# A sliding-window attention with a slot mixture of experts, rewritten with long DMA rows, 96-query blocks and experts in column tiles

## The chip, the cores and the metric

One core of one Trainium2 chip runs the whole program. The metric is the device time of one execution in microseconds (us). An execution is called slow when it lies over 1.5% above the fastest one of the same kernel; verdicts of faster and slower use the other, fast ones. Engines are named as the profile does: PE is the matrix engine, PEld its weight loads, ACT the scalar engine, DVE the vector engine, POOL the engine that issues the casting loads here, SP the one that issues the plain ones. In these kernels PE writes its results to a memory called PSUM, and ACT and DVE carry them from there to SBUF, the working memory of 128 partitions.

## The reference

Eight batches of eight heads with 576 tokens of 64 numbers go through causal attention with a window. Heads 0 to 3 (called plain) see the 32 last tokens, heads 4 to 7 (called dilated) see every fourth of the 128 last. The result, 4608 rows of 512, goes through a soft mixture of experts with 32 slots.

```python
scores = scale * np.matmul(q, k.transpose(0, 1, 3, 2))
mask_plain = (rel >= 0) & (rel < 32)
mask_dil   = (rel >= 0) & (rel < 128) & (rel % 4 == 0)
...                                  # softmax over the masked row, then @ v -> x
logits = x @ phi                     # 4608 x 32
slot_input = softmax(logits, axis=0).T @ x
h = relu(slot_input[e] @ w1[e]);  slot_out[e] = h @ w2[e]      # 8 experts of 4 slots
out = softmax(logits, axis=1) @ slot_out
```

## The kernel before

It works on units of two heads. A load puts token `96 c + p` into partition `p`, so each packet is one token of one head: 256 bytes in HBM, 128 as bf16. PE transposes six 96-token pieces of q and of k, ACT copies each result of 576 columns to SBUF.

```python
# st_dmas: k casts to bf16 on the way in, one token per packet
g.dma_start(kbs[:, :, 64*hx:64*hx+64], k[b, h, 0:576, :].rearrange("(c p) d -> p c d", p=96))
...
# st_transposes and st_evacs, once per unit for q and for k
for c in range(NCH):
    last = pe.transpose(psX_bf[:, 96*c:96*c+96], srcb[:, c, :], ident[0:96, 0:96])
...
ac.activation(dst[:, :], psX_bf[:, 0:S], ACTF.Copy)          # 576 columns, dense
```

After all 32 units come a pass over x for the router (transposes, logits, exponentials, slot sums), a step that scales the token weights, the eight experts one after the other, and the output.

The softmax here doesn't subtract the row's maximum and nothing guards it: scores larger than these inputs give would overflow.

Of the kernel before, what the change touches and what calls it, by code (L numbers as in the profile page):

```python
# [11 lines left out]
N_TOK = B * S  # L13
DM = H * D
E_EXP = 8
SLOTS_PER_E = 4
N_SLOTS = E_EXP * SLOTS_PER_E
FF = 1024
SCALE = 1.0 / (D ** 0.5)
N_TT = N_TOK // 128  # L20
N_G = 9
N_KT = 5

_DBG_UNITS = 0
_DBG_STAGE = 0


class SyncEnv:
# [20 lines left out]
    def now(self, eng):  # L49
        et = eng.engine  # L50
        return (self.ctr_sem[et], self.ctr_val[et])

    def waits(self, eng, evs):
        et = eng.engine
        best = {}
        for ev in evs:
            if ev is None:
                continue
            if isinstance(ev, list):
                sub = ev  # L60
            else:
                sub = [ev]
            for sem, val in sub:
                if val <= 0:
                    continue
                key = sem.num
                if key not in best or val > best[key][1]:
                    best[key] = (sem, val)
        for key, (sem, val) in best.items():
            hw = self.hwm.get((et, key), 0)  # L70
            if val <= hw:
                continue
            eng.wait_ge(sem, val)
            self.hwm[(et, key)] = val


class DmaSem:
# [5 lines left out]
    def inc(self, inst, n=16):  # L83
        inst.then_inc(self.sem, n)
        self.val += n
        return (self.sem, self.val)

    def ev(self):
        return (self.sem, self.val)

    def finals(self):
        return [(self.sem, self.val)] if self.val > 0 else []


class Slot:

    __slots__ = ("ready", "reads")

    def __init__(self):
        self.ready = []  # L100
        self.reads = []

    def war(self):
        return list(self.reads) + list(self.ready)

    def written(self, ev):
        self.ready = [ev] if not isinstance(ev, list) else list(ev)
        self.reads = []


def bass_dilated_sliding_attn__then__soft_moe_slots_kernel(
# [8 lines left out]
    dbg_x=None,  # L120
):
    es = ExitStack()
    A = es.enter_context

    env = SyncEnv(nc)
    WT = env.waits
    SIG = env.sig

    x_sb = A(nc.sbuf_tensor("x_sb", [128, N_TT, DM], BF16))
    xT = A(nc.sbuf_tensor("xT", [128, DM // 128, N_TOK], BF16))  # L130
    w1b = A(nc.sbuf_tensor("w1b", [128, E_EXP, DM // 128, FF], BF16))
    phi_st = A(nc.sbuf_tensor("phi_st", [128, DM // 128, N_SLOTS], F32))
    phi_sb = A(nc.sbuf_tensor("phi_sb", [128, DM // 128, N_SLOTS], BF16))
    ident = A(nc.sbuf_tensor("ident", [128, 128], BF16))
    ident_f = A(nc.sbuf_tensor("ident_f", [N_SLOTS, N_SLOTS], F32))
    mask_plA = A(nc.sbuf_tensor("mask_plA", [128, 448], BF16))
    mask_plB = A(nc.sbuf_tensor("mask_plB", [128, 512], BF16))
    mask_dA = A(nc.sbuf_tensor("mask_dA", [128, 512], BF16))
    mask_dB = A(nc.sbuf_tensor("mask_dB", [128, 512], BF16))

    ps_sc = [A(nc.psum_tensor(f"ps_sc{i}", [128, 512], F32)) for i in range(4)]
    ps_pv = [A(nc.psum_tensor(f"ps_pv{i}", [128, 512], F32)) for i in range(2)]
    ps_ta = A(nc.psum_tensor("ps_ta", [128, 512], F32))
    ps_tb = A(nc.psum_tensor("ps_tb", [128, 512], F32))
    ps_ta_bf = ps_ta[:].bitcast(BF16)
    ps_tb_bf = ps_tb[:].bitcast(BF16)

    att_es = ExitStack()
    AA = att_es.enter_context
    mtmp0 = AA(nc.sbuf_tensor("mtmp0", [128, 512], F32))  # L150
    mtmp1 = AA(nc.sbuf_tensor("mtmp1", [128, 512], BF16))
    mtmp2 = AA(nc.sbuf_tensor("mtmp2", [128, 512], BF16))
    NSLOT = 3
    NVS = 6
    NCH = S // 96
    qs = [AA(nc.sbuf_tensor(f"qs{i}", [96, NCH, 128], F32)) for i in range(NSLOT)]
    qb = [AA(nc.sbuf_tensor(f"qb{i}", [96, NCH, 128], BF16)) for i in range(2)]
    kb = [AA(nc.sbuf_tensor(f"kb{i}", [96, NCH, 128], BF16)) for i in range(NSLOT)]
    vb = [AA(nc.sbuf_tensor(f"vb{i}", [128, 2, 5, D + 1], BF16)) for i in range(NVS)]
    QT = [AA(nc.sbuf_tensor(f"QT{i}", [128, S], BF16)) for i in range(2)]  # L160
    KT = [AA(nc.sbuf_tensor(f"KT{i}", [128, S], BF16)) for i in range(2)]
    NPAR = 6
    pte = [AA(nc.sbuf_tensor(f"pte{i}", [128, 512], BF16)) for i in range(2 * NPAR)]
    pt = [AA(nc.sbuf_tensor(f"pt{i}", [128, 512], BF16)) for i in range(2 * NPAR)]
    rinv = [AA(nc.sbuf_tensor(f"rinv{i}", [128, 8], F32)) for i in range(NPAR)]

    s_in = [DmaSem(nc, f"s_in{i}") for i in range(NSLOT)]
    s_vv = [DmaSem(nc, f"s_vv{i}") for i in range(NVS)]
    s_qs = [DmaSem(nc, f"s_qs{i}") for i in range(NSLOT)]
    s_w1 = DmaSem(nc, "s_w1")  # L170
    s_xT = DmaSem(nc, "s_xT")
    s_phi = DmaSem(nc, "s_phi")
    s_w2 = [DmaSem(nc, f"s_w2_{i}") for i in range(3)]
    s_out = [DmaSem(nc, f"s_out{i}") for i in range(6)]

    blk = A(nc.Block())

    sl_qs = [Slot() for _ in range(NSLOT)]
    sl_qb = [Slot() for _ in range(2)]
    sl_kb = [Slot() for _ in range(NSLOT)]  # L180
    sl_vb = [Slot() for _ in range(NVS)]
    sl_QT = [Slot() for _ in range(2)]
    sl_KT = [Slot() for _ in range(2)]
    sl_pta = Slot()
    sl_ptb2 = Slot()
    sl_pte = [Slot() for _ in range(2 * NPAR)]
    sl_pt = [Slot() for _ in range(2 * NPAR)]
    sl_sc = [Slot() for _ in range(4)]
    sl_pv = [Slot() for _ in range(2)]
    sl_rinv = [Slot() for _ in range(NPAR)]  # L190
    sl_w1 = Slot()
    sl_phi = Slot()
    sl_ident = Slot()
    sl_mask_pl = Slot()
    sl_mask_dl = Slot()

    ev_iota = [None]

    @blk.gpsimd
    def _(g):  # L200
        e0 = SIG(g, g.memset(ident[:], 0.0))
        WT(g, [e0])
        ev_id = SIG(g, g.affine_select(out=ident[:], in_=ident[:],
                                      compare_op=AluOp.not_equal, fill=1.0, base=0,
                                      pattern=[[-1, 128]], channel_multiplier=1))
        WT(g, [ev_id])
        ev_id = SIG(g, g.tensor_copy(ident_f[:, :], ident[0:N_SLOTS, 0:N_SLOTS]))
        sl_ident.written(ev_id)
        ev_iota[0] = SIG(g, g.iota(mtmp0[:], [[1, 512]], base=256, channel_multiplier=-1,
                                   allow_small_or_imprecise_dtypes=True))  # L210
        for i in range(NVS):
            ev = SIG(g, g.memset(vb[i][:, :, :, :], 1.0))
            sl_vb[i].written(ev)
        ins = g.dma_start(phi_st[:], moe_phi.rearrange("(c p) s -> p c s", p=128))
        evp = s_phi.inc(ins)
        WT(g, [evp])
        evc = SIG(g, g.tensor_copy(phi_sb[:], phi_st[:]))
        sl_phi.written(evc)

    @blk.vector  # L220
    def _(vv):
        ev = None
        for pb in ps_sc + ps_pv + [ps_ta, ps_tb]:
            ev = SIG(vv, vv.memset(pb[:], 0.0))
        for s_ in sl_sc + sl_pv + [sl_pta, sl_ptb2]:
            s_.written(ev)
        if _DBG_STAGE:
            SIG(vv, vv.memset(x_sb[:], 0.0))
        WT(vv, [ev_iota[0]])
        e2 = SIG(vv, vv.tensor_scalar(mtmp1[:, 0:192], mtmp0[:, 0:192], 287.0, None, op0=AluOp.is_le))  # L230
        e3 = SIG(vv, vv.tensor_scalar(mtmp2[:, 0:192], mtmp0[:, 0:192], 256.0, None, op0=AluOp.is_ge))
        WT(vv, [e2, e3])
        e4 = SIG(vv, vv.tensor_tensor(mtmp1[:, 0:192], mtmp1[:, 0:192], mtmp2[:, 0:192], AluOp.mult))
        e5 = SIG(vv, vv.memset(mask_plA[:], 0.0))
        e6 = SIG(vv, vv.memset(mask_plB[:], 0.0))
        WT(vv, [e4, e5, e6])
        SIG(vv, vv.tensor_copy(mask_plA[:, 0:160], mtmp1[:, 0:160]))
        SIG(vv, vv.tensor_copy(mask_plA[:, 256:416], mtmp1[:, 0:160]))
        SIG(vv, vv.tensor_copy(mask_plB[:, 0:160], mtmp1[:, 0:160]))
        SIG(vv, vv.tensor_copy(mask_plB[:, 256:416], mtmp1[:, 0:160]))  # L240
        evm = SIG(vv, vv.tensor_copy(mask_plB[0:64, 448:512], mtmp1[0:64, 0:64]))
        sl_mask_pl.written(evm)
        WT(vv, [evm] + sl_ident.ready)
        e8 = SIG(vv, vv.memset(mtmp2[:, 0:256], 0.0))
        e9 = SIG(vv, vv.memset(mtmp1[:, 0:256], 0.0))
# [812 lines left out]
```

## Time and profile before

The median of the first runs was 307 us.

| stage of the kernel before | us | bound by |
|---|---|---|
| start and attention, 32 units | 0 to 183 | arrival of k (and v, q) |
| router | 183 to 218 | PE |
| token weights | 218 to 230 | a chain DVE-PE-DVE |
| experts | 230 to 275 | a chain PE-ACT-PE-DVE |
| output | 275 to 307 | eviction and store |

From the page of the kernel before: busy time by engine, then digits of busy time in tenths for 40 equal slices (PEclk is the granted clock of PE in tenths), and the count of DMA packets.

```profile
PE 208.0 (68%) x2188; PEld 125.2 (41%) x2188; DVE 172.1 (56%) x460; ACT 143.0 (47%) x271; POOL 143.3 (47%) x204
...
ACT  1134848747458566484673827453002334322440
...
PEclk9999999999999999999999999999955999995555
DMA  5899999999999999999999005980000499918896
GB/s 124 69 182 154 196 158 164 185 156 179 169 156 193 156 166 184 156 186 162 158 191 143 6 2 75 196 140 2 0 1 2 65 187 202 207 23 308 322 363 239
DMA packets 131197, 45.56 MB, mean 148 GB/s; under 512 B 115024, under 2 KB 123216, under 8 KB 131168
```

DMA is full (9) through slice 22, but moves mostly 150 to 196 GB/s; seven packets in eight are under 512 bytes. The chain that ended last, in shares of the span, by engine and then by line:

```profile
DMA 40%; PE 31%; POOL 11%; DVE 8%; issue 5%; ACT 3%; ACTq 0%; POOLq 0%; DVEq 0%
DMA kb<-in_k_dram 35%; PE ps_pv L904 5%; DMA out_dram<-ostg 5%; PE ps_sc L852 4%; POOL vb L365 4%; PE ps_pv L499 4%; PE ps_pv L739 3%; POOL w1b L374 2%; POOL kb L358 2%; DVE x_sb L528 2%; PE ps_sc L657 2%; PE ps_sc L826 2%; PE ps_tb L401 2%; PE ps_sc L689 2%; PE ps_sc L436 2%
```

Last, busy time by stage (stretch, its length, then busy us and count of PE, PEld, DVE, ACT and POOL, granted clock, DMA share, GB/s):

```profile
23.00:183.00 160.00, 115.83 (x1587) 84.67 (x1587) 124.87 (x338) 98.27 (x185) 109.14 (x149) 1.00 1.52 155
183.00:218.00 35.00, 31.21 (x277) 17.50 (x273) 13.06 (x39) 15.83 (x36) 2.68 (x3) 1.00 0.57 91
218.00:230.00 12.00, 4.71 (x32) 2.61 (x32) 6.45 (x12) 0.00 (x0) 0.00 (x0) 0.65 0.00 1
230.00:275.00 45.00, 37.41 (x232) 14.68 (x232) 2.44 (x11) 14.07 (x24) 4.37 (x5) 0.90 0.73 117
275.00:308.00 33.00, 16.24 (x36) 3.79 (x36) 11.83 (x18) 9.88 (x18) 6.51 (x12) 0.52 0.74 287
```

### The profile page before, as it was taken

The page shows a single profiled execution, that of the slowest core. Times are in us where ns is not written, and L with a number is a line of the kernel's source. Part 1 is how long each engine was busy: PE and PEld are TensorE (multiplying, and loading weights), DVE is VectorE, ACT ScalarE, POOL GpSimd, SP SyncE. Part 2 cuts the span into 40 slices and gives each one's busy share as a digit, 9 for nine tenths or more (in the row PEclk, how much of TensorE's full clock was granted, in tenths as well). Part 3 has the DMA queues.
Part 4 walks back from the last instruction along what each step waited for, and adds up shares of the span by engine and source line. Part 5 has one row for each costly group of instructions (what it writes and reads, how often), then busy time and mean ns, then how long its engine had stood idle before and what let it go on. Part 6 is the DMA issues. An engine that isn't in the chain of part 4 may idle for free.

```text
span 307.3 us, 5998 instructions
## 1 busy us (share of the span) xinstructions
PE 208.0 (68%) x2188; PEld 125.2 (41%) x2188; DVE 172.1 (56%) x460; ACT 143.0 (47%) x271; POOL 143.3 (47%) x204
## 2 busy tenths in 40 slices
PE   0214958669399595794893969988359898856660
PEld 0102736447267364572563757444132333321110
DVE  8622869959679789496894995332530000023441
ACT  1134848747458566484673827453002334322440
POOL 7998959759479696595990003000000212001221
PEclk9999999999999999999999999999955999995555
DMA  5899999999999999999999005980000499918896
GB/s 124 69 182 154 196 158 164 185 156 179 169 156 193 156 166 184 156 186 162 158 191 143 6 2 75 196 140 2 0 1 2 65 187 202 207 23 308 322 363 239
DMA packets 131197, 45.56 MB, mean 148 GB/s; under 512 B 115024, under 2 KB 123216, under 8 KB 131168
## 3 DMA queue, kind: packets, MB, share of 16 engines
q0 software_dynamic: 89824, 29.44, 82.4%
q1 hardware_dynamic: 39616, 12.59, 25.1%
q10 hardware_dynamic: 1728, 3.15, 2.7%
q8 instruction: 18, 0.29, 0.4%
q14 instruction: 11, 0.09, 0.1%
HBM read 61.93 MB, written 9.44 MB: 232 GB/s over the span
## 4 chain that ended last, share of the span: by engine, by line
DMA 40%; PE 31%; POOL 11%; DVE 8%; issue 5%; ACT 3%; ACTq 0%; POOLq 0%; DVEq 0%
DMA kb<-in_k_dram 35%; PE ps_pv L904 5%; DMA out_dram<-ostg 5%; PE ps_sc L852 4%; POOL vb L365 4%; PE ps_pv L499 4%; PE ps_pv L739 3%; POOL w1b L374 2%; POOL kb L358 2%; DVE x_sb L528 2%; PE ps_sc L657 2%; PE ps_sc L826 2%; PE ps_tb L401 2%; PE ps_sc L689 2%; PE ps_sc L436 2%
## 5 line engine op out<-in xcount | busy, mean ns | idle before, releaser
L452 ACT ACTIVATE pte<-ps_sc 128x512 bf16<-128x512 f32 (+1 forms) x128 | 65.9, 584 | 28.7 <-PE ps_sc L436 28.7
L358 POOL DMA_DIRECT2D kb<-in_k_dram x64 | 49.4, 790 | 27.6 <-PE ps_tb L401 27.5
L528 DVE TENSOR_TENSOR x_sb<-ps_pv,rinv 64x320 bf16<-64x320 f32 (+1 forms) x128 | 58.3, 456 | 4.2
L499 PE MATMUL ps_pv<-vb,pt 128*64 128x65 bf16 (+1 forms) x928 | 51.9, 249 | 2.5 <-DVE x_sb L528 2.5
L401 PE MATMUL ps_tb<-ident,kb 96*128 96x96 bf16 x192 | 21.5, 279 | 45.3 <-DMA kb<-in_k_dram 45.0
L365 POOL DMA_DIRECT2D vb<-in_v_dram x64 | 49.1, 783 | 2.1 <-PE ps_sc L436 1.8
L630 POOL DMA_DIRECT2D w2r<-in_moe_w_dram x8 | 7.1, 884 | 90.5 <-PE ps_ta L879 66.1
L499 PEld LDWEIGHTS ps_pv<-vb,pt 128*64 128x64 bf16 (+1 forms) x928 | 40.8, 150 | 13.8 <-DVE x_sb L528 3.2
L415 ACT ACTIVATE KT<-ps_tb 128x576 bf16<-128x576 bf16 x32 | 21.5, 671 | 34.1 <-PE ps_tb L401 34.1
L436 PE MATMUL ps_sc<-QT,KT 64*128 64x160 bf16 (+3 forms) x320 | 33.3, 342 | 4.0 <-ACT KT L415 2.3
L401 PEld LDWEIGHTS ps_tb<-ident,kb 96*128 96x128 bf16 x192 | 15.8, 138 | 48.9 <-DMA kb<-in_k_dram 48.9
L401 PE MATMUL ps_ta<-ident,qb 96*128 96x96 bf16 x192 | 21.1, 277 | 13.0 <-DVE qb L386 13.0
L415 ACT ACTIVATE QT<-ps_ta 128x576 bf16<-128x576 bf16 x32 | 21.5, 671 | 11.6 <-PE ps_ta L401 11.6
L436 PEld LDWEIGHTS ps_sc<-QT,KT 64*128 64x128 bf16 (+1 forms) x320 | 17.3, 126 | 19.2 <-issue 9.7
L519 DVE RECIPROCAL rinv<-ps_pv 128x5 f32<-128x5 f32 x64 | 12.1, 188 | 22.7 <-PE ps_pv L499 21.8
L1010 POOL DMA_DIRECT2D out_dram<-ostg x12 | 6.5, 544 | 38.0 <-ACT ostg L994 33.8
L889 DVE COPY hT<-ps_ta 128x32 bf16<-128x32 bf16 x8 | 1.4, 174 | 35.9 <-PE ps_ta L879 35.9
L863 ACT ACTIVATE h_sb<-ps_sc 4x512 bf16<-4x512 f32 x12 | 7.0, 586 | 30.9 <-PE ps_sc L852 30.9
L368 POOL DMA_DIRECT2D vb<-in_v_dram x32 | 20.5, 641 | 0.0
L401 PEld LDWEIGHTS ps_ta<-ident,qb 96*128 96x128 bf16 x192 | 14.4, 133 | 15.0 <-issue 12.9
L386 DVE CAST qb<-qs 96x768 bf16<-96x768 f32 x32 | 19.2, 602 | 0.8 <-DMA qs<-in_q_dram 0.8
L467 DVE TENSOR_TENSOR pt<-pte,mask_plA 128x448 bf16<-128x448 bf16 x32 | 12.3, 384 | 11.9 <-ACT pte L452 11.6
(103 smaller groups left out, 268.7 us busy)
## 6 DMA issues: line engine op xcount, KB each, us to landing
qs<-in_q_dram SPq DMA_DIRECT2D x64, 144.0 KB, 9.1
w1b<-in_moe_w_dram POOLq DMA_DIRECT2D x8, 1024.0 KB, 11.8
w2r<-in_moe_w_dram POOLq DMA_DIRECT2D x8, 1024.0 KB, 11.4
kb<-in_k_dram POOLq DMA_DIRECT2D x64, 72.0 KB, 11.6
vb<-in_v_dram POOLq DMA_DIRECT2D x64, 64.0 KB, 11.5
out_dram<-ostg SPq DMA_DIRECT2D x12, 256.0 KB, 2.8
out_dram<-ostg ACTq DMA_DIRECT2D x12, 256.0 KB, 3.3
out_dram<-ostg POOLq DMA_DIRECT2D x12, 256.0 KB, 3.1
```

Of the source, the lines that this page charges most:

```text
L358: ins = g.dma_start(kbs[:, :, 64 * hx:64 * hx + 64], k[b, h, 0:576, :].rearrange("(c p) d -> p c d", p=96))
L365: ins = g.dma_start(vbb[:, hx, 0:4, 0:D], v[b, h, 0:512, :].rearrange("(c p) d -> p c d", p=128))
L368: ins = g.dma_start(vbb[0:64, 0:2, 4, 0:D], v[b, h0:h0 + 2, 512:576, :].rearrange("h p d -> p h d"))
L386: ev = SIG(vv, vv.tensor_copy(qb[tpar][:, :, :], qs[slot][:, :, :]))
L401: last = pe.transpose(psX_bf[:, 96 * c:96 * c + 96], srcb[:, c, :], ident[0:96, 0:96])
L415: ev = SIG(ac, ac.activation(dst[:, :], psX_bf[:, 0:S], ACTF.Copy))
L436: inst = pe.matmul(o_ap, lhsT, rhs, start=True, stop=True)
L452: ev = SIG(ac, ac.activation(hc["pteb"][bi][:, 0:wc], hc["scb"][bi][:, 0:wc], ACTF.Exp, scale=SCALE))
L467: ev = SIG(vv, vv.tensor_tensor(hc["ptb"][bi][:, 0:wc], hc["pteb"][bi][:, 0:wc], mk[:, 0:wc], AluOp.mult))
L499: last = pe.matmul(o_ap, lhsT, rhs, start=(ji == 0), stop=(ji == len(js) - 1))
L528: evn = SIG(vv, vv.tensor_tensor(dst, src, rb, AluOp.mult))
L904: last = pe.matmul(psX[0:SLOTS_PER_E, 0:DM], hT[ep][:, cc, :], w2r[ri][:, cc, :], start=(cc == 0), stop=(cc == 7))
```

## The change

The intent: loads in rows of 6 KB instead of packets of 256 bytes, the router inside the attention loop one batch behind, all experts' weights on chip before they are needed, and each expert in a column tile of 32 so that PE can run several at once.

To get 6 KB rows, 24 neighbouring tokens of a head must lie in one partition. Token `24 p + c` sits in partition `p`, column `c`. A transposition of column `c` then yields tokens 24 apart side by side, and the copy from PSUM has to put them back in order.

```diff
-ins = g.dma_start(kbs[:, :, 64 * hx:64 * hx + 64],
-                  k[b, h, 0:576, :].rearrange("(c p) d -> p c d", p=96))
+res.append(g.dma_start(
+    stg[p0:p0 + NPP, s, 0:6144].rearrange("p (g x) -> p g x", g=4),
+    src[b, half::2, :, :].rearrange("h (p c) d -> p h (c d)", c=PCH)))
 ...
-    last = pe.transpose(psX_bf[:, 96 * c:96 * c + 96], srcb[:, c, :], ident[0:96, 0:96])
-ev = SIG(ac, ac.activation(dst[:, :], psX_bf[:, 0:S], ACTF.Copy))
+def st_A(g, r):                       # four times per half batch, r = 0..3
+    for c1 in range(6):
+        for hx in range(2):
+            i_ = t.transpose(pbf[64 * hx:64 * hx + 64, 128 * c1:128 * c1 + NR],
+                             src[0:NR, 2 * typ + hx, 4 * c1 + r, :], ident[0:NR, 0:NR])
+    pv = pbf[:, 0:768].rearrange("x (c h u) -> x c h u", c=6, h=2)
+    if typ == 0:                      # plain heads: token order
+        d = d.rearrange("x h (p c r) -> x r c h p", c=6, r=4)[:, r]
+    else:                             # dilated heads: the four residues one after the other
+        d = d.rearrange("x h (r p c) -> x r c h p", r=4, c=6)[:, r]
+    ac.activation(d, pv[:, :, :, PCH * t:PCH * t + NPP], ACTF.Copy)
 ... (v the same in st_V; scores, masks, PV in blocks of 96 queries and 128 keys)
+ac.activation(expP[:].rearrange("p (r h s) -> p h s r", r=4, h=2),      # router, per batch
+    lg[:, :, 0:288].rearrange("p h (s r) -> p h s r", r=4), ACTF.Exp)
 ... (first layer: four experts in four column tiles; outputs as rows of 4 KB)
```

## The prediction

> **What bounds it now.** The page gives 307 us. Until 183 us the bound is arrival of q/k/v: the chain of waits is 35% "DMA kb<-in_k_dram", and one k load takes 11.6 us from issue to landing. Of 131,197 DMA packets 115,024 are under 512 B; the 40 slices show DMA at 9 but only 150-195 GB/s. A batch (four units of 5 us) takes 20 us. The Trainium skill, "DMA: Bandwidth & Descriptors", Specifications, asks for 512 B or more; the trace agrees so far as the later weight loads, in large rows, reach 196 GB/s of bf16. By windows: 183-218 us is the router pass (35 us, DMA nearly idle, PE 31 us busy), 218-230 token weights (12), 230-275 the experts one after the other (45), 275-307 output (32).
>
> **Removed.** Small packets; the separate router pass (now inside the attention loop, one batch behind); the token-weight stage (now in the output eviction); the expert-by-expert ping-pong.
>
> **Added per batch, from durations in the trace.**
> - ACT: 34 copies or exponentials, costed from 448 columns = 541 ns and 512 = 599 ns: 288 columns 0.40 us, 576 0.66. 24x0.40 + 10x0.66 = 16.4 us, some 18 with gaps.
> - DVE: four evictions of 768 (0.56), eight mask products (0.45), four reciprocals and normalisations (0.23 + 0.95), four XT copies, one ET copy: 13.5 us, 15 with gaps.
> - PE: about 35 groups of small matmuls. Two 64-column tiles run together (L499: two per 54 ns), a 96-wide transposition costs 80 ns, two 64-row tiles 133 ns, and a change of tile shape costs about 190 ns once (seen between L499, L436 and L401). The skill, "TensorEngine Tiling (Array Packing)", Key Properties, says that changing tiling mode drains the engine; the trace agrees. Sum about 21 us, a third of it group starts and drains.
> - DMA: 2.8 MB as bf16 per batch with one expert of w1; at the 150-200 GB/s seen, 14-19 us.
>
> So the loop turns from DMA-bound to bound by PE with ACT close behind; with two or three PSUM buffers I expect 22-24 us per batch, router included (before 20 + 4.4).
>
> **Sum.** First q/k behind w1's first megabyte and a first transposing step: loop starts at 22 us. 16 steps of 11.3 us: 202. Last batch's router: 212. Tail: first layer 4-5 us if four column tiles overlap (14 if not), ReLU, transposes and row sums 5, second layer 64 matmuls at 216 ns = 14 us (each expert's eight share one column tile, so no overlap), output 9.4 MB at the 320-360 GB/s seen = 28 us. Tail 52 against 89 now. The sum is 264; some waits will overlap: predicted **260 us**, 8 in 10 between 228 and 290. Faster by over 2%: 0.90; within 2%: 0.06; slower: 0.04.
>
> Most of the gain is the tail (37 us).
>
> **What would show it.** Right: packets under 512 B near none; DMA digits of 5-8 in the loop; PE over 85% busy there, its waits short and on ACT or DVE; a batch of 22-24 us; the second layer 14 us; output at DMA 8-9.
>
> **Wrong if:** loads onto only 24 partitions run well under 150 GB/s, so that the loop still waits on DMA (then PE waits on stg, 25 us or more a batch); strided ACT or DVE copies cost more than contiguous ones; PSUM ring waits chain PE-ACT-PE (loop over 26 us a batch); or, the other way, PE overlaps better and ACT sets 18 us a batch (about 225 us).

## More of the kernel before

The two groups of ACT that bring q and k to SBUF, with `xcount | busy us, mean ns of one | idle before`:

```profile
L415 ACT ACTIVATE QT<-ps_ta 128x576 bf16<-128x576 bf16 x32 | 21.5, 671 | 11.6 <-PE ps_ta L401 11.6
L415 ACT ACTIVATE KT<-ps_tb 128x576 bf16<-128x576 bf16 x32 | 21.5, 671 | 34.1 <-PE ps_tb L401 34.1
```

## The result and the profile after

| | median us | runs | ratio to the kernel before, 95% interval |
|---|---|---|---|
| before | 307.35 | 306.93 to 309.76 | |
| changed | 387.78 | 387.31 to 388.03 | 1.2593 (1.2528 to 1.2658) |

A ratio here is the mean time of one kernel's fast runs over that of the other's of the same rounds, so it isn't quite the ratio of the medians. The changed kernel is slower by 26%; the prediction was 260 us, and its range ended at 290. The page of the changed kernel, the same lines as before:

```profile
PE 230.0 (60%) x3056; PEld 170.5 (44%) x3056; DVE 140.6 (36%) x242; ACT 297.6 (77%) x302; POOL 54.5 (14%) x108
...
ACT  1398999799979997999799978997899764120660
...
PEclk9999999999999999999999999999999999999995
DMA  7999994059005900599055005600660066000599
GB/s 138 217 205 213 218 208 90 3 90 205 2 2 83 205 8 2 85 218 205 8 91 95 2 2 108 111 2 0 110 113 2 0 110 111 0 2 2 210 405 364
DMA packets 12623, 40.89 MB, mean 106 GB/s; under 512 B 3633, under 2 KB 3633, under 8 KB 10545
```

The loads did what was wanted. There are 12,623 packets instead of 131,197, they run at 205 to 218 GB/s, where the attention part of the kernel before had 155 in the mean (one slice of it reached 196, so the prediction's 196 alone says little), and DMA then stands idle for one or two slices at a time. ACT took its place: 7 to 9 in every slice of the loop, 298 us busy instead of 143. The chain says the same, 52% ACT and 2% waiting for k:

```profile
ACT 52%; PE 20%; issue 15%; DVE 7%; DMA 2%; POOL 0%; ACTq 0%
ACT VT L378 17%; ACT KT L352 13%; ACT QT L352 12%; ACT PT L419 8%; PE ps_2 L339 2%; DMA stg<-in_k_dram 2%; PE ps_0 L651 2%; DVE XB L447 2%; DVE w1r L676 2%; PE ps_0 L339 2%; PE ps_2 L394 2%; ACT expP L486 1%; PE ps_0 L459 1%; PE ps_0 L599 1%; PE ps_1 L670 1%
```

The ACT groups behind it:

```profile
L378 ACT ACTIVATE VT<-ps_2 128x288 bf16<-128x288 bf16 x30 | 40.9, 1634 | 0.0
L352 ACT ACTIVATE KT<-ps_0 128x288 bf16<-128x288 bf16 x26 | 40.0, 1539 | 0.0
...
L352 ACT ACTIVATE QT<-ps_0 128x288 bf16<-128x288 bf16 x26 | 33.3, 1281 | 14.3 <-PE ps_0 L339 13.8
...
L486 ACT ACTIVATE expP<-ps_0 128x576 bf16<-128x576 f32 x4 | 10.3, 2575 | 0.0
```

The groups are split by PSUM buffer, so the K copies stand there three times in full. A copy has 288 columns now, half of the 576 that took 671 ns, and yet it is listed with 1.3 to 1.7 us. These durations include waiting behind the instruction in front, so starts are the better measure. A stretch of ACT's timeline in the loop (start us, us, what):

```profile
132.69 1.86 ACT L352 ACTIVATE KT<-ps_2 128x288 bf16<-128x288 bf16 x1
134.00 1.02 ACT L419 ACTIVATE PT<-ps_1 128x576 bf16<-128x576 f32 x1
134.89 1.51 ACT L352 ACTIVATE QT<-ps_1 128x288 bf16<-128x288 bf16 x1
135.84 1.87 ACT L352 ACTIVATE KT<-ps_1 128x288 bf16<-128x288 bf16 x1
```

From start to start, a plain Q copy takes 0.95 us (134.89 to 135.84), a K copy 1.3 (132.69 to 134.00); in the trace's dilated copies the medians are 0.73 and 0.97. The prediction had 0.40 for each. By stage (columns as before; the first line is three batches of the loop, then the first layer with its transposes and row sums, the second layer, the output):

```profile
102.00:218.00 116.00, 76.77 (x1080) 60.49 (x1078) 42.10 (x75) 106.40 (x107) 15.98 (x28) 1.00 0.44 83
343.00:350.00 7.00, 6.15 (x107) 3.19 (x100) 1.07 (x3) 1.04 (x3) 0.00 (x0) 1.00 0.00 0
350.00:358.50 8.50, 8.16 (x71) 3.84 (x68) 0.69 (x2) 0.00 (x0) 0.00 (x0) 1.00 0.01 2
358.50:386.00 27.50, 10.75 (x36) 2.15 (x36) 13.14 (x19) 12.03 (x18) 0.00 (x0) 0.82 0.86 343
```

Three batches take 116 us, 38.6 each, and ACT is busy for 106 of them. The prediction had 22 to 24 us per batch. The tail is 43 us (343 to 386), where the prediction had 52 and the kernel before takes 89.

One more reading needs no experiment. The four runs of the changed kernel were granted 0.99, 0.71, 0.72 and 0.60 of PE's clock, and took 387.3, 387.8, 388.0 and 387.7 us. PE at 60% of its clock changes nothing, so PE does not bound the loop of this kernel.

### The profile page after: what moved, and what is told of

Same layout as the page of the kernel before. It is cut to its first block, busy times and chain, and to the rows that moved or that the text cites. A ratio compares the mean times of both kernels' runs of the same rounds, so it can differ in the third digit from the quotient of the medians.

```text
span 385.6 us, 7144 instructions
## 1 busy us (share of the span) xinstructions
PE 230.0 (60%) x3056; PEld 170.5 (44%) x3056; DVE 140.6 (36%) x242; ACT 297.6 (77%) x302; POOL 54.5 (14%) x108
## 2 busy tenths in 40 slices
DMA packets 12623, 40.89 MB, mean 106 GB/s; under 512 B 3633, under 2 KB 3633, under 8 KB 10545
## 4 chain that ended last, share of the span: by engine, by line
ACT 52%; PE 20%; issue 15%; DVE 7%; DMA 2%; POOL 0%; ACTq 0%
ACT VT L378 17%; ACT KT L352 13%; ACT QT L352 12%; ACT PT L419 8%; PE ps_2 L339 2%; DMA stg<-in_k_dram 2%; PE ps_0 L651 2%; DVE XB L447 2%; DVE w1r L676 2%; PE ps_0 L339 2%; PE ps_2 L394 2%; ACT expP L486 1%; PE ps_0 L459 1%; PE ps_0 L599 1%; PE ps_1 L670 1%
## 5 line engine op out<-in xcount | busy, mean ns | idle before, releaser
L352 ACT ACTIVATE QT<-ps_0 128x288 bf16<-128x288 bf16 x26 | 33.3, 1281 | 14.3 <-PE ps_0 L339 13.8
L422 DVE TENSOR_TENSOR PT<-PT,mask_d 128x576 bf16<-128x576 bf16 x32 | 14.7, 459 | 73.9 <-ACT PT L419 73.8
L378 ACT ACTIVATE VT<-ps_2 128x288 bf16<-128x288 bf16 x30 | 40.9, 1634 | 0.0
L352 ACT ACTIVATE KT<-ps_0 128x288 bf16<-128x288 bf16 x26 | 40.0, 1539 | 0.0
L419 ACT ACTIVATE PT<-ps_0 128x576 bf16<-128x576 f32 x32 | 26.2, 820 | 12.8 <-PE ps_0 L413 12.8
L419 ACT ACTIVATE PT<-ps_1 128x576 bf16<-128x576 f32 x32 | 26.4, 826 | 11.4 <-PE ps_1 L413 11.4
L352 ACT ACTIVATE KT<-ps_2 128x288 bf16<-128x288 bf16 x20 | 33.3, 1667 | 0.0
L469 DVE COPY XT<-ps_0 128x576 bf16<-128x576 bf16 x15 | 14.8, 983 | 47.8 <-PE ps_0 L459 47.8
L339 PE MATMUL ps_0<-ident,stg 112*64 112x112 bf16 x312 | 20.1, 300 | 17.1 <-DMA stg<-in_k_dram 15.1
L352 ACT ACTIVATE KT<-ps_1 128x288 bf16<-128x288 bf16 x18 | 28.8, 1602 | 0.0
L352 ACT ACTIVATE QT<-ps_2 128x288 bf16<-128x288 bf16 x20 | 27.8, 1388 | 0.7
L422 DVE TENSOR_TENSOR PT<-PT,mask_p 128x576 bf16<-128x576 bf16 x32 | 14.9, 467 | 32.6 <-ACT PT L419 32.6
L394 PE MATMUL ps_2<-ident,VT 128*128 128x128 bf16 x114 | 15.7, 309 | 16.6 <-ACT VT L378 16.6
L378 ACT ACTIVATE VT<-ps_1 128x288 bf16<-128x288 bf16 x18 | 24.1, 1604 | 0.0
L352 ACT ACTIVATE QT<-ps_1 128x288 bf16<-128x288 bf16 x18 | 24.0, 1331 | 0.0
L339 PEld LDWEIGHTS ps_0<-ident,stg 112*64 112x64 bf16 x312 | 14.6, 164 | 20.7 <-issue 17.1
L378 ACT ACTIVATE VT<-ps_0 128x288 bf16<-128x288 bf16 x16 | 21.5, 1614 | 0.0
L469 DVE COPY XT<-ps_1 128x576 bf16<-128x576 bf16 x16 | 15.6, 975 | 13.5 <-PE ps_1 L459 13.5
L413 PE MATMUL ps_1<-QT,KT 64*128 64x96 bf16 x192 | 13.5, 271 | 10.2 <-ACT KT L352 9.6
```

The source lines that it names most:

```text
L339: i_ = t.transpose(pbf[64 * hx:64 * hx + 64, 128 * c1:128 * c1 + NR], src[0:NR, 2 * typ + hx, 4 * c1 + r, :], ident[0:NR, 0:NR])
L352: return lambda ac: ac.activation(d, pv[:, :, :, PCH * t:PCH * t + NPP], ACTF.Copy)
L378: op("act", lambda ac, d=d, typ=typ: ac.activation(d, pv[:, :, :, PCH * typ:PCH * typ + NPP], ACTF.Copy), r=[pb], **{"w" if r + typ == 0 e ...
L394: i_ = t.transpose(pbf[:, 128 * m:128 * m + 128], VT[:, typ, half, QB * m:QB * m + 128], ident[:, :])
L413: i_ = t.matmul(sc[:, hx, QB * mm:QB * mm + QB], KT[par][64 * hx:64 * hx + 64, half, QB * m:QB * m + 128], QT[par][64 * hx:64 * hx + 64, h ...
L419: op("act", lambda ac: ac.activation(pt[:], sc[:, :, 0:3 * QB], ACTF.Exp, scale=SCALE), r=[scb], w=[ptb])
```

## The experiments

Three theories. **W**: ACT pays for writes that land scattered in SBUF. **R**: ACT pays for reading PSUM in short runs of 24. **C**: ACT is slowed by what other engines or the DMA do at the same time. The kernel before ran at 307.4 us and 307.8.

### Dense writes, dense reads

`dense_write` keeps the reading and writes each copy as two runs of 144; its result is wrong.

```diff
-            if typ == 0:
-                d = d.rearrange("x h (p c r) -> x r c h p", c=6, r=4)[:, r]
-            else:
-                d = d.rearrange("x h (r p c) -> x r c h p", r=4, c=6)[:, r]
+            d = dst[:, :, off:off + S].rearrange("x h (r y) -> x r h y", r=4)[:, r]
```

> Wrong results on purpose: the 24 Q/K/V copies per batch on ACT read PSUM as before but write each 288 elements as two dense runs of 144. Theory W (ACT pays for the scattered 2-byte writes to SBUF, strides of 12 and 48 bytes): a copy falls from 1.0-1.3 us start to start to about 0.4-0.5, ACT busy from 298 to about 165 us, the time to 255-285 us (PE then bounds). Theory R (the price is the reading in short runs of 24 from PSUM): copies and time unchanged, about 386 us. Theory C (contention with PE or DMA): unchanged.

Measured: 276.0 us (slow) and 269.4 (fast). ACT's groups, in the profiled, slow run (busy time and durations of ACT alone are read here):

```profile
L348 ACT ACTIVATE KT<-ps 128x288 bf16<-128x288 bf16 x64 | 27.3, 427 | 0.0
...
L370 ACT ACTIVATE VT<-ps 128x288 bf16<-128x288 bf16 x64 | 20.2, 438 | 6.9 <-PE ps L363 6.9
```

`dense_read` keeps the scattered writes and reads one dense run of 288, also wrong.

```diff
-    pbf[64 * hx:64 * hx + 64, 128 * c1:128 * c1 + NR]
+    pbf[64 * hx:64 * hx + 64, NR * c1:NR * c1 + NR]
-    ac.activation(d, pv[:, :, :, PCH * t:PCH * t + NPP], ACTF.Copy)
+    ac.activation(d, pbf[:, 288 * t:288 * t + 288].rearrange("x (c h p) -> x c h p", c=6, h=2), ACTF.Copy)
```

> Wrong results on purpose: the same copies write scattered as in the changed kernel, but read one dense run of 288 from PSUM. Theory W: no change, 380-388 us. Theory R: copies at 0.4-0.5 us and the time at 255-285 us.

Measured: 387.7 and 388.2 us, and the K copies as in the changed kernel:

```profile
L352 ACT ACTIVATE KT<-ps 128x288 bf16<-128x288 bf16 x64 | 102.1, 1595 | 0.0
```

W holds, R falls. C falls as well: with the other engines busier than before, the densely written copies took 0.43 us.

### The same result with the loops of the copy exchanged

The place of each element need not change to make its neighbour in time its neighbour in SBUF. `loop_swap` runs the innermost loop over `c`. `swap_runs` also lets the plain Q and K heads transpose six neighbouring columns per group, so that they write runs of six too.

```diff
-    "x h (p c r) -> x r c h p"   and   "x h (r p c) -> x r c h p"
+    "x h (p c r) -> x r h p c"   and   "x h (r p c) -> x r h p c"
-    pv[:, :, :, PCH * t:PCH * t + NPP]
+    pv[:, :, :, PCH * t:PCH * t + NPP].rearrange("x c h p -> x h p c")
 swap_runs, st_A only, plain heads:
-    src[0:NR, 2 * typ + hx, 4 * c1 + r, :]        d: "x h (p c r) -> ..."
+    src[0:NR, 2 * typ + hx, 6 * r + c1, :]        d: "x h (p r c) -> x r h p c"
```

> Right results: the same elements go to the same places, but the innermost loop of the copy is over c instead of p: dilated heads write runs of 6 elements (12 bytes), plain heads step 8 bytes; the reading from PSUM steps 256 bytes. Theory W: dilated copies near 0.5 us, plain ones between that and before; time 300-345 us. Theory R: the reading is worse, so slower than 386 us.

> Right results: as loop_swap, and the plain Q/K heads transpose 6 neighbouring columns per group, so that their copies too write runs of 6 elements (12 bytes). Theory W: faster than loop_swap by the plain Q/K copies, 285-330 us. Theory R: as loop_swap, slower than 386 us.

Both gave right results: `loop_swap` 277.3 us in its one fast run and 283.7 to 287.0 in three slow ones (all below the 300 to 345 expected), `swap_runs` 270.2 in its one fast run and 283.7 to 287.5 in three slow ones. Every run of both is below every run of the kernel before. The K copies of the two, first `loop_swap` and then `swap_runs`:

```profile
L352 ACT ACTIVATE KT<-ps 128x288 bf16<-128x288 bf16 x64 | 43.2, 675 | 0.0
```

```profile
L352 ACT ACTIVATE KT<-ps 128x288 bf16<-128x288 bf16 x64 | 27.1, 423 | 0.0
```

So the mean K copy goes 1.6, 0.68, 0.42 us as the writes get denser, while the reading gets more scattered (256 bytes apart). `swap_runs` came out below or at the low end of the 285 to 330 us foreseen; against `loop_swap` its 7 us rest on one run each.

### The disputed cost by itself

`stride_sweep` does no attention. It copies 288 bf16 elements from PSUM on ACT, sixteen copies of each kind, and each copy waits for the end of the one before. `act_w6x` writes at a step of six elements, `act_runs6x` runs of six at 48 bytes, and `act_r` writes dense and reads at steps of 2, 6 and 12.

```python
for s_ in STEPS:                                  # 1, 2, 3, 4, 6, 8, 12, 24
    for _i in range(16):
        ac.activation(wa[s_][:, 0:288 * s_:s_], pbf[:, 0:288], ACTF.Copy)   # then a wait for its end
```

> Wrong results on purpose (it writes zeros): the disputed cost by itself. ACT copies 288 bf16 elements from PSUM, one after the other with nothing else running, to SBUF at steps of 1, 2, 3, 4, 6, 8, 12 and 24 elements, then as runs of 6 at 48 bytes, then reads at steps of 2, 6 and 12 with a dense write; VectorE the same for five write steps. Theory W (the price is a write that lands in another 16-byte line of SBUF than the one before): about 0.4 us for steps 1 to 4, which put two or more elements in a line, then rising at step 6 and flat at 1.1-1.3 us from step 8 on; runs of 6 near 0.5; reads at any step 0.4. Rival W2 (any write that isn't dense costs the same): 1.1-1.3 us already from step 2. Rival C (the price was contention with other engines): 0.4 at all steps.

```profile
L146 ACT ACTIVATE act_w24x<-ps 128x288 bf16<-128x288 bf16 x16 | 23.9, 1491 | 0.5
...
L146 ACT ACTIVATE act_w8x<-ps 128x288 bf16<-128x288 bf16 x16 | 23.1, 1442 | 0.5
L146 ACT ACTIVATE act_w12x<-ps 128x288 bf16<-128x288 bf16 x16 | 22.9, 1431 | 0.5
L154 ACT ACTIVATE act_r<-big 128x288 bf16<-128x288 bf16 x48 | 19.7, 411 | 1.5
L146 ACT ACTIVATE act_w6x<-ps 128x288 bf16<-128x288 bf16 x16 | 18.0, 1126 | 0.5
...
L146 ACT ACTIVATE act_w4x<-ps 128x288 bf16<-128x288 bf16 x16 | 12.9, 808 | 0.5
...
L146 ACT ACTIVATE act_w3x<-ps 128x288 bf16<-128x288 bf16 x16 | 10.4, 648 | 0.5
L146 ACT ACTIVATE act_w2x<-ps 128x288 bf16<-128x288 bf16 x16 | 7.9, 491 | 0.5
...
L150 ACT ACTIVATE act_runs6x<-ps 128x288 bf16<-128x288 bf16 x16 | 6.6, 411 | 0.5
L146 ACT ACTIVATE act_w1x<-ps 128x288 bf16<-128x288 bf16 x16 | 6.6, 411 | 0.5
```

| step, bytes | 2 | 4 | 6 | 8 | 12 | 16 | 24 | 48 |
|---|---|---|---|---|---|---|---|---|
| lines of 16 bytes touched | 36 | 72 | 108 | 144 | 216 | 288 | 288 | 288 |
| ns | 411 | 491 | 648 | 808 | 1126 | 1442 | 1431 | 1491 |

From 72 lines up the time is a straight line: (808 - 491) / 72 = 4.4 ns and (1442 - 808) / 144 = 4.4 ns per line of 16 bytes, plus about 0.17 us. Beyond 16 bytes it stays flat. Runs of six cost what a dense copy costs, and the three reading steps cost nothing (411 ns in the mean). VectorE has the same price: in the same kernel it took 307, 478, 795, 1112 and 1477 ns for steps of 1, 2, 4, 6 and 24 elements.

W was right about the place of the cost and wrong about its shape: steps of 2 to 4 elements were expected to be free and are not. W2 (anything not dense costs the same) falls too. The Trainium skill, "SBUF — State Buffer", Specifications (TRN2), gives lines of 16 bytes and a penalty for each move to another; the sweep agrees. It also asks for at least two hits per line for full bandwidth; two were not enough in the sweep, where two per line (a step of 8 bytes) took 808 ns against 411.

An estimate with this price explains the loop. Per batch the 16 Q and K copies touch 8 x 288 + 8 x 216 = 4032 lines and the eight V copies 4 x 288 + 4 x 216 = 2016; 6048 x 4.4 ns = 26.6 us. The permuted exponential adds 576 lines, 2.5 us, the eight score exponentials 8 x 0.65 = 5.2 and the other router exponential 0.85. The sum is 35 us; measured, 106.4 / 3 = 35.5. The 0.17 us per copy is left out, since in the loop a copy starts before the one in front has ended.

### One exponential

`expp_order` is the changed kernel with one loop exchanged, that of the router's permuted exponential.

```diff
-    expP[:].rearrange("p (r h s) -> p h s r", r=4, h=2),
-    lg[:, :, 0:288].rearrange("p h (s r) -> p h s r", r=4), ACTF.Exp),
+    expP[:].rearrange("p (r h s) -> p h r s", r=4, h=2),
+    lg[:, :, 0:288].rearrange("p h (s r) -> p h r s", r=4), ACTF.Exp),
```

> Right results: the changed kernel with one alteration, the permuted exponential of each batch writes runs of 72 and reads PSUM at 16 bytes, where it wrote every element 288 bytes from the last. Theory W: the exponential falls from 2.58 us to about 0.8, ACT busy by 14 us; as ACT bounds the loop, the time by 8 to 14 us, to 373-380. Rival (the permuted reading costs as much): no change.

Measured: 372.4 us (372.2 to 373.1), ratio 1.2151 to the kernel before. It was 2575 ns:

```profile
L486 ACT ACTIVATE expP<-ps 128x576 bf16<-128x576 f32 x8 | 5.2, 654 | 0.0
```

ACT lost 15.0 us (297.6 to 282.6 busy) and the time fell by 15.3, just more than the 8 to 14 expected. (The two kernels ran in different calls; by their ratios to the kernel before the gain is 13.6 us.) In this loop a microsecond saved on the bounding engine is about a microsecond of the whole.

### The same fault put into the kernel before

```diff
-ac.activation(dst[:, :], psX_bf[:, 0:S], ACTF.Copy)
+ac.activation(dst[:, :].rearrange("p (a b) -> p b a", a=24),
+              psX_bf[:, 0:S].rearrange("p (b a) -> p b a", a=24), ACTF.Copy)
```

> Wrong results on purpose: the kernel before, with its 64 QT/KT copies of 576 elements writing each element 48 bytes from the last. Theory W: a copy goes from 0.67 to 2.1-2.6 us, ACT per unit from 3.7 to 6.6-7.6 us against 5.0 us of DMA pace, so the attention part grows from 160 to 210-245 us and the time to 355-395 us. Rival C (something of the new kernel slows ACT): 307 us as before.

Measured: 400.6 and 403.4 us, ratio 1.3108 (two runs; the verdict is given as unclear). ACT's copies went from 671 ns to:

```profile
L415 ACT ACTIVATE KT<-ps_tb 128x576 bf16<-128x576 bf16 x32 | 101.4, 3169 | 1.1 <-PE ps_tb L401 1.1
```

ACT went from 143 to 278 us busy, 2.1 us more for each of the 64 copies, so some 2.8 us a copy; the 3.17 listed include waiting. The time is above the range expected: 576 lines at 4.4 ns and 0.17 us make 2.7 us a copy, a price which I had not yet measured. The scattered write alone, without anything else of the rewrite, turns the kernel before into a slower one than the changed kernel. This run carries a warning as well. It permutes the tokens of q and k and is still judged correct. Worked out from the reference's inputs, not from a run, no scaled score is larger than 0.061 in size, so the softmax is nearly flat under its mask, and the permutation changes the output by 0.2%. So the comparison says little about the order of q and k. For `loop_swap` and the kernels after it, that order rests on the index maps, where each element goes to the place that it had.

### All writes dense, and what bounds then

`all_runs` is `swap_runs` with `expp_order`'s exchange and the same one in DVE's XT copies (the transposed x for the router) of the dilated heads. `v_dense` takes it as base and lets the last scattered copies, the plain heads' V at steps of 8 bytes, write runs of 12 bytes. Its output is wrong, which doesn't matter for the time. `qkv_first` issues the first q/k/v loads ahead of the first expert's weights. `first_grouped` adds to that a new order of PE's groups, with fewer changes of tile shape (the rows and columns of PE's array that a matmul uses). `all_runs_again` is `all_runs` once more, beside the last three.

```diff
 all_runs, XT copy:
-    d.rearrange("p (s r) -> p r s", r=4)  <-  pbf[:, 0:S].rearrange("p (r s) -> p r s", r=4)
+    d.rearrange("p (s r) -> p s r", r=4)  <-  pbf[:, 0:S].rearrange("p (r s) -> p s r", r=4)
 v_dense, st_V, plain heads:
-    "x h (p c r) -> x r h p c"
+    "x h (r p c) -> x r h p c"
 qkv_first:
-    load_w1(0); ...; load_qkv(0); load_w1(1)
+    ...; load_qkv(0); load_w1(0); load_w1(1)
 first_grouped, per half batch (S scores, A transpositions):
-    S00 A0 S01 A1 ...  S10 A2 S11 A3
+    S00 S01 A0 A1 ...  S10 S11 A2 A3      (the router's group that stood after A2 moves behind A3)
```

> Right results: swap_runs with the permuted exponential and the two XT copies of the dilated heads also writing dense. Theory W: ACT busy about 136 us, DVE 125; the time at best as dense_write's fast run, 262-280 us, now set by PE, whose granted clock was 0.66-0.76 in the last runs; faster than before by 9-15%.

> The same kernel as all_runs, as the base for the other three of this call on one chip: 248-259 us as before.

> Wrong results on purpose: all_runs with the plain heads' V copies, the last ones that write at steps of 8 bytes, made to write runs of 12 bytes. ACT loses 32 times 0.4 us, 13 us. If PE bounds the loop now, as the prediction said it would, the time falls by under 5 us; if ACT still does, by about 10 to 13 us.

> Right results: all_runs with the first q/k/v loads issued ahead of the first expert's weights. The first transposition waited 15 us for k behind 1 MB; it should start about 5 us earlier and the whole end 4 to 6 us earlier, 243-254 us. If the start is hidden, no change.

> Right results: qkv_first with the score groups and the transposition groups of each half step put in pairs, so that PE changes its tile shape less often (four changes fewer of about twelve per step of half a batch). If a change costs PE about 0.1-0.2 us and PE bounds the loop, 5 to 10 us less than qkv_first; if the interleaving was hiding ACT's latency, slower by some us.

| run | median us | runs | ratio of fast runs |
|---|---|---|---|
| all_runs | 253.5 | 248.3 to 258.6 (one of six fast) | none given |
| all_runs_again | 254.3 | 251.0 to 256.9 (two of four fast) | 0.8173 |
| v_dense (wrong result) | 245.0 | 243.8 to 246.8 (all fast) | 0.7941 |
| qkv_first | 257.1 | 253.9 to 262.7 (three of four fast) | 0.8313 |
| first_grouped | 245.5 | 243.8 to 250.8 (three of four fast) | 0.7954 |

The means of the fast runs of the last four are 251.7, 245.1, 256.0 and 244.9 us, and the differences below are between these.

`all_runs` is right and takes 18% less time than the kernel before. It also came out below the 262 to 280 us expected: ACT and DVE were not only shorter, PE waited for them less (for the permuted exponential 6 us in `all_runs_again`, 22 in `swap_runs`, both slow).

`v_dense` took away 6.6 us where ACT lost 11.3, between the two answers expected. So PE alone does not bound the loop: the eight V copies come in one burst per batch, and PE waits in it. PE's idle time before the V transpositions and before the group that reads their copies fell from 8.0 us (`all_runs_again`, slow) to 3.1. `qkv_first` missed: its fast runs are 4.3 us slower than those of `all_runs_again`. Its first transposition began at 15.2 us, that of `all_runs_again` at 15.1. The trace shows why: the first q load waits for DVE to clear the staging buffer and is issued at 4.4 us in both, and the weights had been loading in the idle time before. Now they load between the first q/k/v and the next, and PE waits 4.6 us for the second batch's k (to 34.5 us), a wait that `all_runs_again` doesn't have. `first_grouped` gained 11.1 us on `qkv_first`, a little more than expected, though it keeps 3.7 us of that wait. PE is busy for 171 us in its profile; `v_dense`, the fast profile with the old order, has 184. (`qkv_first` has 195, but was profiled at a clock of 0.74, so its busy time can't be compared.) It is the best right version. Its busy times and its chain:

```profile
PE 171.3 (70%) x3055; PEld 132.0 (54%) x3056; DVE 131.8 (54%) x242; ACT 132.9 (55%) x302; POOL 54.9 (23%) x108
...
PE 46%; DVE 20%; ACT 11%; DMA 9%; issue 6%; POOL 3%; ACTq 0%
```

Its loop and its tail:

```profile
23.00:201.00 178.00, 140.57 (x2754) 117.85 (x2755) 104.39 (x204) 112.22 (x264) 36.17 (x70) 0.81 0.82 158
201.00:244.00 43.00, 25.15 (x207) 9.20 (x200) 14.90 (x23) 13.07 (x21) 0.00 (x0) 0.86 0.55 220
```

The loop is 178 us, 22.3 per batch, with PE busy for 141 us; PE leads the chain with 46%. The granted clock of PE is 0.81 in this loop and 1.00 in that of the kernel before. Why the clock differs was not tested and stays open.

## Why the prediction was wrong, point by point

- **"288 columns about 0.40 us, 576 0.66"**: this is the step that failed. Both sizes came from dense copies of the kernel before, which has no scattered copy to read a price from. A dense copy of 288 does take 0.41 us (sweep), but the change writes scattered, and those copies took 0.73 to 1.3 us of ACT each from start to start, the permuted exponential 2.6. ACT per batch was 35.5 us, not 16.4.
- **"Wrong if: strided ACT or DVE copies cost more than contiguous ones"** named the risk without a size. The diff shows the steps (48 and 12 bytes), and the Trainium skill, "SBUF — State Buffer", Specifications (TRN2), names the line of 16 bytes; neither was put into the sum.
- **"22-24 us per batch"**: 38.6 in the changed kernel. With only the orders of columns and copies exchanged, `all_runs` has 190 us for the loop, 23.8 per batch, in a slow run: PE 20.1 (predicted 21), ACT 14.7 (16.4), DVE 12.9 (13.5). It ends at 248 to 252 us in the fast runs, against the 260 predicted. So the other terms of the loop were about right, and one term carried the miss.
- **"PE over 85% busy, its waits short"**: PE was busy for 77 of 116 us and waited on ACT. The fall of PE's clock to 0.60 without any effect shows it off the bound. With dense writes it came near: 161 of 190 us, 85%, in `all_runs` (slow).
- **"Loads onto only 24 partitions"** were feared; they ran at 205 to 218 GB/s and no wait of the loop was on them. Packets under 512 bytes fell from 115,024 to 3,633, which isn't "near none".
- **DVE "13.5 us"**: 14.0 (42.1 / 3), nearly right, though the same cost was in it. The dilated heads' XT copies wrote every element 8 bytes from the last; an XT copy was listed with 0.98 us in the mean, and with 0.60 in `all_runs`.
- **The tail, "52 us"**: 43. First layer and output as predicted (5 and 27.5 us). ReLU, transposes and row sums took some 2.3 us, not 5, and the second layer 8.0, not 14: "no overlap" was wrong. Its matmuls start in pairs, the next expert's beside this expert's, though each expert's eight follow one another in the program. PE's timeline, where `w2r` is an earlier expert than `stg`:

```profile
351.86 0.39 PE L651 MATMUL ps_0<-stg,hT 128*32 128x512 bf16 x1
352.07 0.38 PE L651 MATMUL ps_0<-w2r,hT 128*32 128x512 bf16 x1
```

- **"A change of tile shape costs about 190 ns"**: `first_grouped` fits that. It has 64 changes fewer (four in each of 16 half batches), 12.2 us at this price, and gained 11.1 us; PE's busy time is 13 us below that of `v_dense`. That no other effect of the order is in it was not separated.

## What to carry to other kernels

When a change makes DMA rows longer by putting neighbouring tokens into one partition, look at who has to put them back in order: count the 16-byte lines that each copy touches, and price a copy by the larger of its elements (0.41 us for 288 alone, 0.29 from start to start in a row of copies in `first_grouped`) and its lines (4.4 ns each). If that hurts, exchange the loops of the copy so that the scattered side is the read from PSUM, which was free here at every step tried (4 to 24 bytes in the sweep, 256 in `swap_runs`). And price a term by a duration of the same access pattern, not only of the same size; where the trace has none, let that set the width of the range.

## What the Trainium skill lacked or had wrong

- "SBUF — State Buffer", Specifications (TRN2): the page asks for two hits or more per 16-byte line for full bandwidth, and two are not enough. A write of two bf16 elements per line took 808 ns for 288, a dense one 411; two or three per line (every 6 bytes, 108 lines) still took 648. The runs fit 4.4 ns per line touched.
- "ScalarE: Activation LUTs" gives no price for a scattered write; the sweep gives 411 to 1491 ns for one and the same copy. VectorE has the same slope (478 ns for 72 lines, 1477 for 288).
- "PSUM — Partial Sum Buffer", Specifications (TRN2), says that a pattern that isn't contiguous slows matmuls; that ACT may read PSUM at steps of 4, 12 and 24 bytes for nothing (411 ns) is on no page.
- "TensorE: Matmul & The Clock Gate", Part 3, The mechanism, says that matmuls start and end in program order. In the second layer, in different column tiles, a later expert's matmul started at 351.86 us and an earlier expert's at 352.07; 64 matmuls of 512 columns took 8.0 us, where one after the other takes 216 ns each.
